# Moving the K/V ring of a decode-attention kernel to a different start address in SBUF

## The chip, the cores and the metric

The kernel runs on one core of one Trainium2 chip. The metric is device time in microseconds (us). A run counts as slow when it is over 1.5% above the fastest of the same kernel. Single executions of one kernel mostly agree within 0.3%, and the quantity studied here is about half a per cent, so the experiments were timed in five rounds against the kernel before on the same chip (three chips in all).

Terms: HBM is the chip's main memory and SBUF the core's working memory, in 128 partitions. Transfers (DMA) from HBM to SBUF run on 16 DMA engines. PE multiplies matrices, DVE is the vector engine, ACT takes the exponential, POOL does some of the small work. A row is the contiguous piece that a transfer writes into one partition; in the trace it is one DMA packet.

## The reference

One token attends to a cache of 65536 keys and values (8 KV heads, 16 query heads, head size 256, bf16), the result goes through an output matrix, and a small gated MLP is mixed in. Cut to what matters:

```python
def _A_ref(x, k_cache, v_cache, wq, wo):        # k_cache, v_cache: [1, 8, 65536, 256] bf16
    q = (x @ wq) ...                            # 16 query heads
    scores = einsum("bhqd,bhkd->bhqk", q, k) * (Dh ** -0.5)
    p = softmax(scores)
    o = einsum("bhqk,bhkd->bhqd", p, v)
    return o... @ wo
g = sigmoid((x * gate_w).sum(-1, keepdims=True))
return g * a + (1 - g) * b                      # a: attention, b: the MLP
```

K and V together are 537 MB (8 x 65536 x 256 x 2 B, twice). Each byte is read once and used for very little arithmetic.

## The kernel before

K and V stream through a ring of four buffers of 4 MiB. An item is one chunk of K or V of one head. In each of the 128 partitions it is one contiguous row of 32768 B, in HBM as well as in SBUF. Where the ring starts in SBUF follows from the order in which the pools are opened: the constants come first.

```python
SB = 16; SIZES = (4,) * 8; RING = 4; MAXS = max(SIZES)       # 4 * 16 * 256 * 2 B = 32768 B
...
const = ctx.enter_context(tc.tile_pool(name="const", bufs=1))
ringp = ctx.enter_context(tc.tile_pool(name="ring", bufs=1))
work = ctx.enter_context(tc.tile_pool(name="work", bufs=1))
...
ring = [ringp.tile([128, MAXS * SB * DH], BF16, name=f"ring{i}") for i in range(RING)]
...
def piece(item, j, n):
    i, is_v = divmod(item, 2)
    g, c = divmod(i, n_chunks)
    nb = sizes[c] * SB
    lo = sum(sizes[:c]) * SB * 128
    src = (A_v_cache if is_v else A_k_cache)[0, g, lo:lo + 128 * nb, :]
    src = src.rearrange("(p j) d -> p (j d)", j=nb)
    nc.sync.dma_start(
        out=ring[item % RING][:, j * DH:(j + n) * DH], in_=src[:, j * DH:(j + n) * DH]
    )
# ... (the last two items come in smaller pieces)
# per chunk: DVE transposes K (turn), PE makes scores, ACT the exponential, PE multiplies with V,
# and as soon as a buffer has been used, load(item + RING) refills it
```

In the program that this builds, the four buffers start at 45696, 78464, 111232 and 144000 bytes into each partition. All four are 128 B past a multiple of 512 (45696 = 89 x 512 + 128).

The softmax here doesn't subtract the row's maximum and nothing guards it: scores larger than these inputs give would overflow.

Of the kernel before, what the change touches and what calls it, by code (L numbers as in the profile page):

```python
# [8 lines left out]
FP32 = mybir.dt.float32  # L9
# [24 lines left out]
def kernel(  # L34
# [28 lines left out]

    ctx.enter_context(tc.manual_schedule())

    const = ctx.enter_context(tc.tile_pool(name="const", bufs=1))
    ringp = ctx.enter_context(tc.tile_pool(name="ring", bufs=1))
    work = ctx.enter_context(tc.tile_pool(name="work", bufs=1))
    psum = ctx.enter_context(tc.tile_pool(name="psum", bufs=1, space=bass.MemoryType.PSUM))

    ring = [ringp.tile([128, MAXS * SB * DH], BF16, name=f"ring{i}") for i in range(RING)]

    sc = [psum.tile([128, 512], FP32, name=f"sc{i}") for i in range(2)]
# [406 lines left out]
```

## Time and profile before

The median was 1282.75 us over three runs (1282.71 to 1283.07).

| part | busy | share of the span |
|---|---|---|
| K/V queue of the 16 DMA engines | | 98.4% |
| PE matmuls | 754.8 us | 59% |
| DVE | 661.4 us | 52% |
| ACT, POOL | 62.6, 82.9 us | 5%, 6% |

These are lines of the page of the profile of the kernel before: busy time by engine, then the span in 40 equal slices (a digit is the busy share in tenths), then the queues with packets, MB and share, and the chain of waits by engine.

```profile
span 1280.9 us, 10091 instructions
PE 754.8 (59%) x4374; PEld 287.3 (22%) x4374; DVE 661.4 (52%) x429; ACT 62.6 (5%) x159; POOL 82.9 (6%) x118
...
DMA  9999999999999999999999999999999999999996
GB/s 392 430 432 428 433 432 425 431 434 428 433 429 428 430 436 425 428 436 425 433 430 427 431 435 427 429 432 429 431 431 429 429 431 434 429 431 432 427 432 270
DMA packets 21154, 544.88 MB, mean 425 GB/s; under 512 B 2675, under 2 KB 2806, under 8 KB 3958
...
q1 hardware_dynamic: 19730, 540.55, 98.4%
...
DMA 64%; DVE 17%; PE 16%; issue 2%; DVEq 0%; SPq 0%; ACT 0%; ACTq 0%
```

The row of nines is the main thing: the DMA engines are busy 90% or more in every slice but the last, and between the first slice and the last the rate is flat (425 to 436 GB/s). So the transfers set the time, and a change matters only if it changes what a transfer costs or how long the engines wait for the next. The chain also has DVE and PE in it (33%), which could mislead: they are the links by which a buffer comes free. The issue table, whose last number is the time from issue to landing, shows that this is not where time is lost:

```profile
ring_69<-in_A_k_cache_dram SPq DMA_DIRECT2D x32, 4096.0 KB, 27.2
ring_70<-in_A_v_cache_dram SPq DMA_DIRECT2D x32, 4096.0 KB, 30.7
ring_71<-in_A_k_cache_dram SPq DMA_DIRECT2D x31, 4096.0 KB, 28.5
ring_72<-in_A_v_cache_dram SPq DMA_DIRECT2D x31, 4096.0 KB, 34.0
```

A 4 MiB transfer needs 9.75 us at 430 GB/s, but it lands 27 to 34 us after its issue. By these figures it spends most of that time queued behind about two others, so a next one is ready.

The same in two stretches of 600 us (busy us of PE, PE weight loads, DVE, ACT and POOL, then granted PE clock, DMA share, GB/s):

```profile
40.00:640.00 600.00, 351.43 (x1982) 131.91 (x1982) 309.54 (x186) 36.53 (x86) 67.80 (x70) 0.86 1.00 430
640.00:1240.00 600.00, 364.53 (x2035) 137.22 (x2033) 304.29 (x177) 21.31 (x62) 2.31 (x3) 0.84 1.00 430
```

The trace also records each DMA packet with its size and duration. For a row of 32768 B (16128 of them, 1008 for each of the 16 engines) the mean was 1219.9 ns, the median 1218 ns and the shortest 1213 ns.

### The profile page before, as it was taken

The page shows a single profiled execution, that of the slowest core. Times are in us where ns is not written, and L with a number is a line of the kernel's source. Part 1 is how long each engine was busy: PE and PEld are TensorE (multiplying, and loading weights), DVE is VectorE, ACT ScalarE, POOL GpSimd, SP SyncE. Part 2 cuts the span into 40 slices and gives each one's busy share as a digit, 9 for nine tenths or more (in the row PEclk, how much of TensorE's full clock was granted, in tenths as well). Part 3 has the DMA queues.
Part 4 walks back from the last instruction along what each step waited for, and adds up shares of the span by engine and source line. Part 5 has one row for each costly group of instructions (what it writes and reads, how often), then busy time and mean ns, then how long its engine had stood idle before and what let it go on. Part 6 is the DMA issues. An engine that isn't in the chain of part 4 may idle for free.

```text
span 1280.9 us, 10091 instructions
## 1 busy us (share of the span) xinstructions
PE 754.8 (59%) x4374; PEld 287.3 (22%) x4374; DVE 661.4 (52%) x429; ACT 62.6 (5%) x159; POOL 82.9 (6%) x118
## 2 busy tenths in 40 slices
PE   3564556754566555756566565665655655656646
PEld 2121222221222222212122122221222222222212
DVE  7364445554464644546445455454453644545545
ACT  0000000000000000000000000000000000000000
POOL 3111002111021110110000000000000000000000
PEclk9888878888789888898888887888977888879789
DMA  9999999999999999999999999999999999999996
GB/s 392 430 432 428 433 432 425 431 434 428 433 429 428 430 436 425 428 436 425 433 430 427 431 435 427 429 432 429 431 431 429 429 431 434 429 431 432 427 432 270
DMA packets 21154, 544.88 MB, mean 425 GB/s; under 512 B 2675, under 2 KB 2806, under 8 KB 3958
## 3 DMA queue, kind: packets, MB, share of 16 engines
q1 hardware_dynamic: 19730, 540.55, 98.4%
q0 software_dynamic: 1376, 3.69, 0.8%
q8 instruction: 34, 0.56, 0.2%
q14 instruction: 10, 0.08, 0.0%
q10 hardware_dynamic: 4, 0.00, 0.0%
HBM read 544.22 MB, written 0.00 MB: 425 GB/s over the span
## 4 chain that ended last, share of the span: by engine, by line
DMA 64%; DVE 17%; PE 16%; issue 2%; DVEq 0%; SPq 0%; ACT 0%; ACTq 0%
DMA ring_69<-in_A_k_cache_dram 58%; PE sc_73 L351 13%; DVE kT_182 L343 9%; DVE kT_183 L343 7%; DMA ring_71<-in_A_k_cache_dram 6%; PE sc_74 L351 1%; DVE acc L334 1%; PE misc L399 1%; PE misc L409 1%; PE misc L322 0%; DVE acc L414 0%; PE pv_76 L373 0%; DVE pT_187 L362 0%; DVE oT L403 0%; DVEq L343 0%
## 5 line engine op out<-in xcount | busy, mean ns | idle before, releaser
L351 PEld LDWEIGHTS <-qw 128*128 128x128 bf16 x2048 | 222.2, 111 | 779.7 <-issue 322.5
L351 PE MATMUL sc_73<-kT_182,qw 128*128 128x512 bf16 x512 | 188.9, 533 | 246.0 <-DVE kT_182 L343 246.0
L343 DVE STREAM_TRANSPOSE kT_182<-ring_69 128x2048 f32<-128x2048 f32 x64 | 147.6, 2306 | 171.1 <-DMA ring_69<-in_A_k_cache_dram 151.2
L351 PE MATMUL sc_74<-kT_182,qw 128*128 128x512 bf16 x512 | 147.5, 437 | 118.5 <-DVE kT_182 L343 118.0
L343 DVE STREAM_TRANSPOSE kT_182<-ring_71 128x2048 f32<-128x2048 f32 x64 | 147.0, 2296 | 120.2 <-DMA ring_71<-in_A_k_cache_dram 93.9
L351 PE MATMUL sc_73<-kT_183,qw 128*128 128x512 bf16 x512 | 148.3, 439 | 25.1 <-DVE kT_183 L343 25.1
L343 DVE STREAM_TRANSPOSE kT_183<-ring_71 128x2048 f32<-128x2048 f32 x64 | 145.7, 2277 | 3.4 <-DMA ring_71<-in_A_k_cache_dram 1.6
L343 DVE STREAM_TRANSPOSE kT_183<-ring_69 128x2048 f32<-128x2048 f32 x64 | 145.5, 2273 | 2.5 <-PE sc_73 L351 2.5
L351 PE MATMUL sc_74<-kT_183,qw 128*128 128x512 bf16 x512 | 130.7, 398 | 17.7 <-DVE kT_183 L343 17.7
L362 DVE STREAM_TRANSPOSE pT_186<-p_184 128x512 bf16<-128x512 bf16 x32 | 22.8, 711 | 100.9 <-ACT p_184 L358 100.9
L362 DVE STREAM_TRANSPOSE pT_187<-p_185 128x512 bf16<-128x512 bf16 x32 | 22.8, 711 | 86.7 <-ACT p_185 L358 86.7
L358 ACT ACTIVATE p_184<-sc_73 128x512 bf16<-128x512 f32 x32 | 19.1, 597 | 714.9 <-PE sc_73 L351 714.9
L373 PE MATMUL pv_75<-ring_70,pT_186 128*4 128x512 bf16 x512 | 30.4, 379 | 24.4 <-DVE pT_186 L362 24.4
L373 PE MATMUL pv_76<-ring_70,pT_186 128*4 128x512 bf16 x512 | 30.4, 379 | 24.4 <-DVE pT_186 L362 24.4
L373 PEld LDWEIGHTS <-pT_186 128*4 128x4 bf16 x1024 | 22.1, 87 | 87.3 <-DVE pT_186 L362 64.6
L358 ACT ACTIVATE p_185<-sc_74 128x512 bf16<-128x512 f32 x32 | 19.1, 597 | 454.0 <-PE sc_74 L351 454.0
L373 PE MATMUL pv_75<-ring_72,pT_187 128*4 128x512 bf16 x512 | 30.4, 379 | 18.3 <-DVE pT_187 L362 18.3
L373 PE MATMUL pv_76<-ring_72,pT_187 128*4 128x512 bf16 x512 | 30.4, 379 | 18.3 <-DVE pT_187 L362 18.3
L373 PEld LDWEIGHTS <-pT_187 128*4 128x4 bf16 x1024 | 22.1, 86 | 71.3 <-DVE pT_187 L362 48.4
L334 DVE SCALAR_TENSOR_TENSOR acc<-misc,half_g,acc 1x448 f32<-1x448 f32 x14 | 9.4, 671 | 53.1 <-PE misc L322 53.1
L311 POOL TENSOR_SCALAR t_b<-t_b 128x448 f32<-128x448 f32 x14 | 7.9, 564 | 357.7 <-ACT t_b L303 357.7
L136 POOL DMA_DIRECT2D wo_96<-in_A_wo_dram x4 | 3.1, 784 | 301.7 <-PE misc L409 301.7
(90 smaller groups left out, 200.8 us busy)
## 6 DMA issues: line engine op xcount, KB each, us to landing
ring_69<-in_A_k_cache_dram SPq DMA_DIRECT2D x32, 4096.0 KB, 27.2
ring_70<-in_A_v_cache_dram SPq DMA_DIRECT2D x32, 4096.0 KB, 30.7
ring_71<-in_A_k_cache_dram SPq DMA_DIRECT2D x31, 4096.0 KB, 28.5
ring_72<-in_A_v_cache_dram SPq DMA_DIRECT2D x31, 4096.0 KB, 34.0
ring_71<-in_A_k_cache_dram SPq DMA_DIRECT2D x4, 1024.0 KB, 28.5
ring_72<-in_A_wq_dram SPq DMA_DIRECT2D x1, 3072.0 KB, 10.1
ring_72<-in_A_v_cache_dram SPq DMA_DIRECT2D x3, 1024.0 KB, 27.7
wo_95<-in_A_wo_dram POOLq DMA_DIRECT2D x4, 448.0 KB, 15.7
```

The lines of the kernel that those rows point to most:

```text
L136: nc.gpsimd.dma_start(out=wo_t[g % 2][:], in_=A_wo[g * 512:(g + 1) * 512, :].rearrange("(q p) n -> p q n", p=128),)
L311: nc.gpsimd.tensor_scalar(out=t_b[:], in0=t_b[:], scalar1=GELU_C1, scalar2=1.0, op0=ALU.mult, op1=ALU.add)
L334: nc.vector.scalar_tensor_tensor(out=acc[:], in0=misc[0:1, 0:D], scalar=half_g[0:1, 0:1], in1=acc[:], op0=ALU.mult, op1=ALU.add,)
L343: nc.vector.transpose(out=kT[n % 2][:].bitcast(FP32), in_=kn[:, s * SB * 128:(s + 1) * SB * 128])
L351: nc.tensor.matmul(sc[i % 2][:], lhsT=qw[:, g, q, PAD - s:PAD - s + 128], rhs=kv[:, :, q // 2, :, q % 2], start=(s == 0 and q == 0), stop= ...
L358: nc.scalar.activation(out=p_t[i % 2][:], in_=sc[i % 2][:], func=ACT.Exp, scale=scale, accum_out=den[g % 2][:, c:c + 1],)
L362: nc.vector.transpose(out=pT_t[i % 2][:], in_=p_t[i % 2][:])
L373: nc.tensor.matmul(pv[g % 2][32 * a:32 * a + 4, :], lhsT=pT[:, k, :, s], rhs=vt[:, j * DH:(j + 2) * DH], start=first and k < 4, stop=last ...
L399: nc.tensor.matmul(o_ps[:, 2 * c:2 * c + 2], lhsT=pvs[:, lo:lo + 128], rhs=sel[:, 2 * half:2 * half + 2], start=(half == 0), stop=(half == 1),
L409: nc.tensor.matmul(a_ps, lhsT=oT[:, 2 * c + r:2 * c + r + 1], rhs=wo_t[g % 2][:, 2 * r + c, :], start=(c == 0 and r == 0), stop=(c == 1 an ...
```

## The change

Its intent: "The K/V ring allocated first, so that every row a transfer writes begins at a multiple of 512 bytes in SBUF". The diff without its blank lines:

```diff
+    ringp = ctx.enter_context(tc.tile_pool(name="ring", bufs=1))
     const = ctx.enter_context(tc.tile_pool(name="const", bufs=1))
-    ringp = ctx.enter_context(tc.tile_pool(name="ring", bufs=1))
     work = ctx.enter_context(tc.tile_pool(name="work", bufs=1))
     psum = ctx.enter_context(tc.tile_pool(name="psum", bufs=1, space=bass.MemoryType.PSUM))
+    ringp.tile([128, 96], FP32, name="pad")
     ring = [ringp.tile([128, MAXS * SB * DH], BF16, name=f"ring{i}") for i in range(RING)]
```

The padding is needed because other data reach up to 16512 = 32 x 512 + 128; the 384 B of the pad take the ring to 16896 = 33 x 512. No instruction is added, removed or reordered. Every other tile moves as well: the transposed K tiles, for instance, went from 128 to 0 past a multiple of 512.

## The prediction

> **What bounds the kernel.** The transfers. The 40-slice row shows the 16 DMA engines at 90% or more in every slice but the last, at 425 to 436 GB/s between the first slice (392) and the last (270). The queue table gives the K/V queue 98.4% of 16 engines' span. PE is busy 59%, DVE 52%. The chain of waits is 64% DMA; DVE (17%) and PE (16%) are links in it, but transfers queue about three deep: one of 4 MiB lands 27 to 34 us after its issue and needs only 9.7 us at 430 GB/s. So the engines are never short of work, and the time is their sum: the transfer records hold 16128 rows of 32768 B, 1219.9 ns on average (median 1218, fastest 1213), 1008 per engine = 1229.6 us; all packets of that queue make 1260 us per engine.
>
> **What the change does.** Nothing is added, removed or reordered; each engine's instruction order is the same. Only addresses move: the four ring buffers began 128 B past a multiple of 512 in each partition (45696 = 89 x 512 + 128), now at a multiple (16896 = 33 x 512). All other tiles move too; their transfers and operations are not on the critical path.
>
> **Cost.** One can only gain what a row takes above its floor. The Trainium skill, "DMA: Bandwidth & Descriptors", section "Where 436 GB/s comes from", gives 435.2 GB/s for 16 ports, 27.2 each; a row at that rate is 1204.7 ns (estimate from that page). Our median row runs at 26.9, so alignment can give at most 13 ns a row, 1.1%, about 14 us. The same page, "How a descriptor splits into AXI transactions", says that a descriptor not starting at a multiple of 256 B begins with a transaction whose unused bytes still cost beats. At 128 B off that is 4 beats of 32 B, 4.7 ns per row (estimate, if it holds for the writing side): 1008 rows, about 5 us.
>
> Against it: very different packets take about the same excess over that floor. In the transfer records rows of 3072 B and 5120 B take 121 and 196 ns (8 over), 8192 B 309 (8), and the output weights' packets of 4480 B, made of five 896 B rows at odd offsets, at best 173 (8, not five times that). So most of the excess looks fixed per packet, not due to the start address. A cost for each 512 B block is unlikely: rows already run at 99% of the port rate.
>
> I give no effect (0 to 1 ns per row) about half, 4 to 5 ns about a quarter, the rest to values between and to the full 13.
>
> **Predicted time:** 1280.0 us, 8 in 10 between 1272 and 1284. Faster by over 2%: 1%; within 2%: 98%; slower by over 2%: 1%.
>
> **What would show it.** Right: the same 40-slice row, median 32768 B row 1213 to 1218 ns, time changed by about 1.05 us per ns of row time; K transposes at about 2.28 us and matmuls as before; the 12 us tail unchanged. Wrong: rows near 1205 ns (alignment was the whole excess), or DMA slices below 9 (then feeding, not row time, matters).
>
> **What would make it wrong.** A write path that splits every block at 512 B and hides it only partly; a second ceiling than the ports; moved kT or query tiles slowing DVE or PE enough to delay ring release.

## The result, and the profile after

The changed kernel took 1276.91 us (median of four runs, 1276.85 to 1277.04), against 1282.73 us for the kernel before (four runs). The ratio is 0.9954, with a 95% interval of 0.9937 to 0.9971. Here and below a ratio is the mean time of one kernel's fast runs over that of the other's of the same rounds, so it is not quite the ratio of the medians quoted. The gain, 5.8 us, is clear of noise and well inside 2%.

The same lines of the page after:

```profile
span 1275.1 us, 10091 instructions
PE 758.4 (59%) x4374; PEld 288.1 (23%) x4374; DVE 661.7 (52%) x429; ACT 62.7 (5%) x159; POOL 83.1 (7%) x118
...
DMA  9999999999999999999999999999999999999996
GB/s 393 434 431 430 436 432 427 436 433 430 435 430 430 433 434 432 432 434 428 433 435 427 435 433 430 432 434 430 431 435 431 430 433 435 430 433 435 428 433 276
DMA packets 21154, 544.88 MB, mean 427 GB/s; under 512 B 2675, under 2 KB 2806, under 8 KB 3958
...
q1 hardware_dynamic: 19730, 540.55, 98.5%
...
DMA 64%; DVE 17%; PE 17%; issue 2%; DVEq 0%; SPq 0%; ACT 0%; ACTq 0%
```

The two stretches after:

```profile
40.00:640.00 600.00, 355.87 (x1992) 133.15 (x1992) 311.29 (x187) 36.55 (x86) 68.34 (x70) 0.86 1.00 432
640.00:1240.00 600.00, 362.46 (x2024) 136.41 (x2023) 303.72 (x178) 21.33 (x62) 2.31 (x3) 0.85 1.00 432
```

The picture is the same: as many packets, as many bytes, engines just as full. Only the rate went from 430 to 432 GB/s. It is in the rows' own durations. From the transfer records, the 32768 B rows by duration:

```
                    up to 1213 ns   1214-1217   1218-1225   over 1225    mean     median
kernel before            21%           27%         46%         6%       1219.9    1218
changed kernel           96%            0%          1%         3%       1215.1    1213
```

After the change nearly every row takes exactly 1213 ns. Before, a fifth did; 70% took 1 to 9 ns more. Over all rows of 3000 B and more in the K/V queue (1096 for each engine) the sum per engine went from 1259.19 to 1254.21 us, 5.0 us less. The span is 5.75 us shorter. The rest divides into 0.6 us less between the rows (from the first row's start to the last row's end, less the rows' own time) and 0.16 us less between the last row's end and the end of the kernel.

The compute side did not change. The transposes of K out of the first ring buffer, before (durations are min/median/max in ns):

```profile
L343 DVE STREAM_TRANSPOSE kT_182<-ring_69 x64: 2289/2311/2315, 23.3 to 1250.6; 128x2048 f32<-128x2048 f32 x64
L343 DVE STREAM_TRANSPOSE kT_183<-ring_69 x64: 2256/2269/2312, 25.5 to 1252.9; 128x2048 f32<-128x2048 f32 x64
```

and after (the names count one higher, because of the pad tile):

```profile
L346 DVE STREAM_TRANSPOSE kT_183<-ring_70 x64: 2289/2311/2314, 23.3 to 1245.0; 128x2048 f32<-128x2048 f32 x64
L346 DVE STREAM_TRANSPOSE kT_184<-ring_70 x64: 2256/2269/2314, 25.5 to 1247.3; 128x2048 f32<-128x2048 f32 x64
```

The medians are equal to the nanosecond, although both source and destination moved. So where a tile lies made no difference to DVE here.

### The profile page after: what moved, and what is told of

It is laid out like the page before. It is cut to its first block, busy times and chain, and to the rows that moved or that the text cites. A ratio compares the mean times of both kernels' runs of the same rounds, so it can differ in the third digit from the quotient of the medians.

```text
span 1275.1 us, 10091 instructions
## 1 busy us (share of the span) xinstructions
PE 758.4 (59%) x4374; PEld 288.1 (23%) x4374; DVE 661.7 (52%) x429; ACT 62.7 (5%) x159; POOL 83.1 (7%) x118
## 4 chain that ended last, share of the span: by engine, by line
DMA 64%; DVE 17%; PE 17%; issue 2%; DVEq 0%; SPq 0%; ACT 0%; ACTq 0%
DMA ring_70<-in_A_k_cache_dram 58%; PE sc_74 L354 14%; DVE kT_183 L346 9%; DVE kT_184 L346 7%; DMA ring_72<-in_A_k_cache_dram 6%; PE sc_75 L354 1%; PE misc L402 1%; DVE acc L337 1%; PE misc L412 1%; PE misc L325 0%; DVE acc L417 0%; PE pv_77 L376 0%; DVE pT_188 L365 0%; DVE oT L406 0%; DVEq L346 0%
```

## The experiments

Three questions were open. Is it the start address, or something else that the new order moved? Is the unit 512 B, as the change says? And what is the price: is it paid per row or per block, for writing or for reading, and does it grow with the distance from the boundary? The theory with which I started was the one in the prediction, that a row pays the bytes between the last multiple of 256 B and its start. Its rivals were that the order matters, that 512 B is the unit, that any start off a multiple pays a fixed price, and that what counts is whether source and destination differ.

### 1 and 2: address or order

In `e1_old_order_aligned` the pools keep the old order and only the address is mended (ring at 46080 = 90 x 512):

```diff
 # before, pools in the old order
+    ringp.tile([128, 96], FP32, name="pad")
     ring = [ringp.tile(...) ...]
```

> The old order of the pools (constants first), but 384 B of padding inside the ring pool so that the ring begins at 46080 = 90 x 512. If the start address of the rows is the cause: as the changed kernel, 1276.9 us, ratio to before 0.9955, and 32768 B rows nearly all at 1213 ns. If the cause is that the ring comes first (where the constants, kT and query tiles ended up): as before, 1282.7 us, ratio 1.000, rows at 1213 to 1222 ns.

Measured: 1277.49 us, ratio to before 0.9954. 96% of the rows took 1213 ns.

In `e2_ring_first_128` the order is the new one and only the address is spoilt (17024 = 33 x 512 + 128):

```diff
 # changed kernel
-    ringp.tile([128, 96], FP32, name="pad")
+    ringp.tile([128, 128], FP32, name="pad")
```

> The new order of the pools, but 512 B of padding in place of 384, so that the ring begins 128 B past a multiple of 512 again. If the start address is the cause: 1282.7 us, ratio 1.000, rows spread from 1213 to 1222 ns with a mean about 1217 in undisturbed transfers. If the order is the cause: 1276.9 us, ratio 0.9955.

Measured: 1282.87 us, ratio 0.9996. The rows have the histogram of before to within two percentage points (21%, 28%, 45%, 6%) and its mean of 1219.9 ns.

It is the start address of the ring, all of it. The order of the pools is worth nothing in itself, and the first experiment is the smaller way to write the change: one line.

### 3: the unit

("The skill's rule", here and in the ninth experiment, is the rule of the unused bytes that the prediction cites; a beat is its step of 32 B.)

```diff
-    ringp.tile([128, 96], FP32, name="pad")
+    ringp.tile([128, 160], FP32, name="pad")      # ring at 17152 = 33 x 512 + 256
```

> Ring first, beginning 256 B past a multiple of 512. If multiples of 256 B are enough (the skill's rule of the 256 B transaction, on the writing side): as the changed kernel, 1276.9 us, rows at 1213 ns. If 512 B is the unit that counts: slower than that, as before or worse, 1282.7 us or up to 1289 us (8 beats, 9.4 ns a row, an estimate).

Measured: 1277.32 us, ratio 0.9952, 96% of rows at 1213 ns. So 512 is not the unit: a start at an odd multiple of 256 B is as good.

### 4, 5 and 6: does the price grow with the distance?

The pad is 112, 104 or 144 words, so the ring starts 64, 32 or 192 B past a multiple of 512.

```diff
-    ringp.tile([128, 96], FP32, name="pad")
+    ringp.tile([128, 112], FP32, name="pad")      # + 64;  104: + 32;  144: + 192
```

> Ring first, beginning 64 B past a multiple of 512. If each row pays the bytes between the last multiple of 256 B and its start, in beats of 32 B: 2 beats, 2.4 ns a row, half of the loss of 128 B, 1279.5 to 1280 us. If each row pays a fixed price for any start off the multiple (one more transaction): 1282.7 us as with 128. If starts at multiples of 64 B are fine: 1276.9 us.

> Ring first, beginning 32 B past a multiple of 512. Beats theory (a row pays the bytes below its start in beats of 32 B): 1 beat, 1.2 ns a row, 1278.6 us. Fixed theory (any start off 256 B makes one more transaction at a fixed price of 4 to 5 ns a row): 1282 to 1283 us, as with 64 and 128.

> Ring first, beginning 192 B past a multiple of 512. Beats theory: 6 beats, 7.1 ns a row, 1284.5 to 1285 us, above before. Fixed theory: 1282 to 1283 us.

All starts, by distance from the last multiple of 256 B (medians; the row means are from the transfer records; the last column is an estimate, from the prediction's 4.7 ns for 4 beats):

| start past a multiple of 256 B | time, us | ratio to before | mean 32768 B row, ns | bytes-below-the-start theory, ns more |
|---|---|---|---|---|
| 0 (changed kernel, run again as e12) | 1277.40 | 0.9956 | 1215.2 | 0 |
| 0 (e3, 256 past 512) | 1277.32 | 0.9952 | 1215.2 | 0 |
| 32 (e5) | 1284.00 | 1.0003 | 1220.9 | 1.2 |
| 64 (e4) | 1281.95 | 0.9992 | 1218.7 | 2.4 |
| 128 (e2) | 1282.87 | 0.9996 | 1219.9 | 4.7 |
| 192 (e6) | 1281.93 | 0.9989 | 1218.7 | 7.1 |

My theory falls: 32 B should have been the cheapest of the four and has the dearest mean, and 192 B should have been the dearest and is, with 64 B, the cheapest. Each start off a multiple of 256 B costs 3.5 to 5.7 ns per row on average. That is closer to a fixed price than to one that grows, though not quite one price. Part of the difference lies in few slow rows: without the rows over 1225 ns (3% when aligned, 5 to 6% here) the price is 3.7 ns at 64, 128 and 192 B and 4.7 ns at 32 B. By the median row the order is another: 2 ns more at 64 and 192, 3 at 32, 5 at 128. The share of rows that pay nothing (1213 ns) is 7% at 64 and 192, 1% at 32 and 21% at 128.

Some caution with the times: single executions here sometimes come out about 2 us longer with no difference in clock (four of the nine runs of before beside e5 and e6 took 1285.0 to 1285.3, the other five 1282.7 to 1283.1), so the intervals of these ratios overlap. One such execution was profiled (e10 below, 1285.06 us). Its rows are those of before; what is longer is the end, 8.8 us in place of 7.0 after the last row, where the last 32 matmuls with V took 3.56 us in place of 1.90. In the timeline of e10:

```profile
1273.70 3.56 PE L378 MATMUL pv<-ring,pT 128*4 128x512 bf16 x32
```

and of the kernel before:

```profile
1272.92 1.90 PE L373 MATMUL pv_76<-ring_72,pT_187 128*4 128x512 bf16 x32
```

So this scatter, at least there, is not in the transfers. The order of the four rests on the median times and on the rows' means, one profile each, which agree. For 64 and 192 B they agree to 0.02 us and to the tenth of a ns.

### 7 and 8: per row or per byte?

Each 4 MiB load is cut into four of 8192 B per row, once with the ring at a multiple of 512 and once 128 B past it.

```diff
 # in piece(); the second run has the 512 B pad of e2 as well
-        nc.sync.dma_start(
-            out=ring[item % RING][:, j * DH:(j + n) * DH], in_=src[:, j * DH:(j + n) * DH]
-        )
+        parts = 4 if n == MAXS * SB else 1
+        w = n // parts * DH
+        for h in range(parts):
+            q = j * DH + h * w
+            nc.sync.dma_start(
+                out=ring[item % RING][:, q:q + w], in_=src[:, q:q + w]
+            )
```

> The changed kernel (ring at a multiple of 512), each 4 MiB load cut into four of 8192 B per row. The baseline for the next run. From the 309 ns that 8192 B rows took in the changed kernel against 1213 for 32768 B: 4 x 309 - 1213 = 23 ns more per 32 KB, times 992 to 1008 rows an engine: about 23 us, 1300 us, if the engines stay fed.

> As the run before, with the ring 128 B past a multiple of 512. If the price is paid once per row of a transfer: four times as many rows, so about four times the loss of 5.8 us, 16 to 23 us above the run before. If it is paid per byte or per 256 B block: the same loss as with long rows, about 6 us above the run before.

Measured: 1294.05 us (ratio 1.0086) and 1314.73 us (ratio 1.0238; four executions). By the medians the misaligned start costs 20.7 us here against 5.8 us with long rows. Both kernels scatter by over 3 us (1293.81 to 1297.51 and 1312.16 to 1315.63); between the two profiled executions, which both have a long end like the one described above (9.7 and 9.5 us after the last row), the difference is 17.7 us. The sum of the rows per engine, which does not depend on the end, grows by 19.3 us against 5.0 with long rows: 3.9 times as much for 3.8 times as many rows (4120 against 1096 an engine), over the same bytes. The price is paid per row. Lines of the page of e7:

```profile
DMA  9999999999999999999999999999999999999995
DMA packets 75592, 544.95 MB, mean 421 GB/s; under 512 B 8723, under 2 KB 8854, under 8 KB 10006
```

and of e8:

```profile
DMA  9999999999999999999999999999999999999995
DMA packets 75592, 544.95 MB, mean 415 GB/s; under 512 B 8723, under 2 KB 8854, under 8 KB 10006
```

Packets and fullness are equal and only the rate differs, so this is row time and not a wait for something to do. In the records an 8192 B row takes 309.6 ns on average when aligned and 314.3 ns at 128 B: 4.7 ns, the same as for a row of 32768 B (1219.9 - 1215.2 = 4.7). This does not hold for every length: the 128 rows each of 3072 and 5120 B at the end of the kernel before, at the same 128 B past, paid 0.8 and 1.8 ns on average.

The first of the two misses its expected time: 1300 us were expected and 1294 came. Rows of 309 ns were right (their sum grew by 23.3 us an engine), but the extra rows' time was not all extra span. The time between the rows (as defined above, which also counts other queues' packets) fell from 12.35 to 5.5 us when there were four times as many, and I have not looked into why.

### 9 and 10: reading or writing?

Two kernels with wrong values read every row, except those of the last two loads, 128 B further on in HBM. The destination is at a multiple of 512 in e9 and 128 B past it in e10 (the 512 B pad of e2 as well).

```diff
-        src = (A_v_cache if is_v else A_k_cache)[0, g, lo:lo + 128 * nb, :]
-        src = src.rearrange("(p j) d -> p (j d)", j=nb)
+        flat = (A_v_cache if is_v else A_k_cache).rearrange("b h s d -> (b h s d)")
+        at = (g * SK + lo) * DH + (SRC if i < total - 1 else 0)       # SRC = 64 elements
+        src = flat[at:at + 128 * nb * DH].rearrange("(p x) -> p x", p=128)
```

> Wrong values on purpose (every row but those of the last two loads is read 128 B further on in HBM). Ring at a multiple of 512, source rows 128 B off. If only where a row is written counts: 1276.9 to 1277.5 us, rows at 1213 ns. If the skill's rule holds for reads (a first transaction with 4 unused beats): 1281 to 1283 us. If what counts is whether source and destination differ modulo 256 B: 1283 us, rows spread 1213 to 1222 ns.

> Wrong values on purpose. Source and destination rows both 128 B off. If only the written address counts: 1282.9 us. If the difference between the two counts: 1277 us. If reads and writes each pay: up to 1288 us.

Measured: e9 took 1277.46 us (ratio 0.9957), with 96% of rows at 1213 ns, like the changed kernel. e10 took 1283.03 us (ratio 1.0001), with the histogram of before (21%, 28%, 45%, 6%). The comparison with the reference does not see such a shift; that does not touch the timing. The two stretches of e9 (columns as above, the last is GB/s):

```profile
40.00:640.00 600.00, 356.39 (x1992) 133.89 (x1992) 310.33 (x187) 36.66 (x87) 68.45 (x70) 0.85 1.00 432
640.00:1240.00 600.00, 364.07 (x2026) 137.60 (x2024) 303.66 (x178) 21.31 (x62) 2.31 (x3) 0.84 1.00 432
```

and of e10:

```profile
40.00:640.00 600.00, 352.11 (x1982) 131.23 (x1982) 309.22 (x186) 36.66 (x87) 68.45 (x70) 0.86 1.00 430
640.00:1240.00 600.00, 364.63 (x2019) 137.31 (x2021) 304.42 (x177) 21.31 (x62) 2.31 (x3) 0.84 1.00 431
```

Of the two addresses only the one in SBUF that is written counts, as far as a shift of 128 B can show it. Moving the read address by 128 B costs nothing here. (Where the caches start in HBM is not on record, so the source's own distance from a multiple of 256 B is not known.) Shifting both alike does not help, so it is not a matter of the two being out of step. The profile of e10 is that of its longest execution (1285.06 us); the extra 2 us are at the end, as said above.

### 11 and 12: fewer, longer rows

If a row has a fixed price, longer rows should save some of it. Three buffers of 6 blocks replace four of 4; the last run is the changed kernel again, on the same chip.

```diff
-SIZES = (4,) * 8
-RING = 4
+SIZES = (6, 6, 5, 5, 5, 5)
+RING = 3
```

> The changed kernel with chunks of 6, 6, 5, 5, 5, 5 blocks in place of eight of 4, and three ring buffers in place of four: rows of 49152 and 40960 B, 768 in place of 1024 an engine for all of K and V. If a row costs a fixed price beside its bytes (5.6 ns of time per extra row, from cutting rows in four: (1294.05 - 1277) us / 3024), about 1.4 us less than the changed kernel, 1275.5 us; if three buffers leave the engines waiting, slower, with DMA slices under 9.

> The changed kernel itself, as the baseline on this chip: ratio to before 0.9954, 1277 us.

Measured: e11 took 1278.69 us (ratio 0.9969) and e12 1277.40 us (ratio 0.9956). The expected gain of 1.4 us did not come. The typical rows behaved: medians of 1514 ns for 40960 B and 1815 ns for 49152 B. The sums in the profiles, against those of the changed kernel: 856 in place of 1096 rows per engine, but their total only 0.33 us shorter (1253.88 against 1254.21), because more of them were slow (mean 1828 ns at 49152 B, where the median is 1815); 1.3 us more between the rows; and 0.7 us more after the last row. The last is plain in the timeline of the end: the last P times V product has five blocks in place of four and ran 4.08 us in place of 2.04. In e11:

```profile
1266.68 4.08 PE L376 MATMUL pv<-ring,pT 128*4 128x512 bf16 x40
```

and in the changed kernel:

```profile
1267.05 2.04 PE L376 MATMUL pv_77<-ring_73,pT_188 128*4 128x512 bf16 x32
```

40 matmuls in place of 32 do not explain a doubling by themselves; the remainder is that each ran slower here, about 102 ns in place of 64. That is no mark of the long rows: the last 32 matmuls took 3.3 us in the profiles of e7 and e8 and 3.6 in that of e10, and 1.9 to 2.6 in the others. What makes them slow at times, and why more rows were slow, stays open. A difference of 1.3 us, with runs that scatter by 2 us (1278.12 to 1281.38), should not be read further. The changed kernel is not beaten by it.

## Why the prediction was right or wrong

- **What bounds the kernel: right.** The slices stay at nine in every kernel that was run, and the time follows the rows. Both the gain and the loss in e8 were in the row durations.
- **Nothing else moves: right.** The old order with an aligned ring gave all of the gain (0.9954) and the new order with a misaligned ring none (0.9996). K transposes kept their 2311 and 2269 ns.
- **The bound on the gain: kept, and useful.** The row that cannot be beaten was put at 1204.7 ns (an estimate), so at most 1.1% was to be had. Aligned rows stopped at 1213 ns. No run shows whether less is possible.
- **The time: inside the range, but 3.1 us too high** (1280.0 against 1276.9). The range, 1272 to 1284, also held no effect at all, so being inside it says little; the 1280.0 lies between the two effects that were weighed. The failed step is the paragraph "Against it". From small packets that took about 8 ns over the floor I concluded that "most of the excess looks fixed per packet, not due to the start address", and gave no effect about half the weight. About 8 ns is indeed what an aligned row of K or V still has over the estimated floor (1213 - 1204.7), at 3072 B (121 ns) as at 49152 B (1815 ns). But I compared the medians or minima of the small packets with a big row whose mean was 1219.9, and what lay between the fastest row and the mean was, for the most part, the price in question: 4.8 of 6.9 ns. The small rows had it too. The 309 ns quoted for 8192 B were the fastest of 896 such rows in the kernel before; their median was 313 and their mean 313.8, and after the change the mean was 309.6. The 5120 B and 3072 B rows at the end averaged 197.8 and 121.8 ns before, and 196.0 and 121.0 after. The spread above the minimum was the clue, in a trace where most rows can repeat to the nanosecond, as the one after the change shows.
- **The size, 4.7 ns per row and "about 5 us": right in number (4.7 to 4.8 ns, 5.0 us), by a wrong reason.** It was computed from unused bytes below the start. Then 32 B should have cost 1.2 ns and cost 5.7, and 192 B should have cost 7.1 and cost 3.5. The rule was given for the reading side; on that side, a shift of 128 B cost nothing (e9). That the number came out was luck.
- **"About 1.05 us per ns of row time": right for the rows, low for the whole.** The rows' sum fell by 5.0 us for 4.8 ns, 1.05 us per ns. The time fell by 5.8 us, because 0.6 us came from between the rows and 0.2 us from the end.
- **What stays open:** why a start off 256 B costs what it does (3.5 ns at 64 and 192, 4.7 at 128, 5.7 at 32), why a fifth of the rows at 128 B pay nothing, and why rows of 3072 and 5120 B paid less. One more access at each row, because a row that starts off a boundary touches 129 blocks of 256 B in place of 128, would fit a price per row and the unit of 256 B, but not these differences; no run separates it from other causes, and it was not tried whether the row's start or its end pays.

## What to carry to other kernels

Where a kernel is bound by transfers whose rate is already flat, first estimate the most that can be gained per row (here 13 ns in 1218), and then look at the spread of row durations: here most of the scatter above the shortest row was a price that could be saved. Start the SBUF rows of big loads at multiples of 256 B. It costs one line of padding, and here it was worth 0.5% with rows of 32 KB and 1.3 to 1.6% (17.7 us by the profiles, 20.7 us by the medians) with rows of 8 KB, because the price is per row; a source address 128 B further on and the place of other tiles did not matter.

## What the Trainium skill lacked or had wrong

- "DMA: Bandwidth & Descriptors", section "How a descriptor splits into AXI transactions", counts the unused bytes of a read and does not say what a start off 256 B costs where SBUF is written: rows written 32, 64, 128 or 192 B past a multiple of 256 B took 3.5 to 5.7 ns more each on average, while a source in HBM moved by 128 B cost nothing (1277.46 us against 1277.40). Carried over to the writing side, its count of unused bytes does not give the sizes: 32 B had the dearest mean and 192 B one of the two cheapest.
- "SBUF — State Buffer", section "Operand start alignment", treats legality and says that its runs timed nothing. For the speed of these loads 256 B was the unit: an odd multiple of 256 was as good as a multiple of 512 (1277.32 us against 1277.40), and 32, 64, 128 and 192 B were not.
- The DMA page's figures of a fixed cost per packet are given for small packets (sections "Measured (HBM→SBUF, 128 partitions, SWDGE, issued from GpSimd)" and "Why small descriptors are slow (HBM only)"); none is a measured time for a long row. Here an aligned row of K or V typically took about 8 ns over its bytes at that page's port rate (an estimate), at every length that was run: 121 ns for 3072 B, 309 for 8192 B, 1213 for 32768 B, 1815 for 49152 B.
- The same DMA page, section "Where 436 GB/s comes from", says that for loads from HBM the HBM side, about 358 GB/s per core, is what limits. A note above it keeps that figure for two busy cores that share an HBM, and the section should say so too: with one core used by the program, this kernel loaded at 432 GB/s over 1200 us, just under the 435 GB/s of the ports.
